# Turning float64 weights into fp32 on VectorE and ScalarE instead of GpSimd, and computing a branch's flag beside the last block

## The chip, the core and the metric

The kernel runs on one core of a Trainium2 chip. The metric is the device time of one execution in microseconds (us). The engines are named as in the profile: PE (TensorE, the matmuls), PEld (its weight loads), DVE (VectorE), ACT (ScalarE), POOL (GpSimd) and SP (SyncE, which here issues the input DMAs). Each engine works through its own list of instructions in order, and waits at an instruction until the semaphores that it names have been raised.

## The reference

A gated linear recurrence over the sequence, followed by a feed-forward block on its output. Cut to what is computed:

```
q, k, v, f_logit: (4, 8, 768, 48) float32      # batch, heads, sequence, head width
f = sigmoid(f_logit)
for t in range(768):
    state = f[t][:, None] * state + outer(k[t], v[t])   # per batch and head, 48 x 48
    y[t] = q[t] @ state
x = y as (3072, 384)                            # tokens x (heads * width)
g = x @ w_gate;  out = (g * sigmoid(g) * (x @ w_val)) @ w_out
w_gate, w_val: (384, 1536), w_out: (1536, 384), all three float64
```

The weights come as float64 (two 32-bit words each), and the kernel makes fp32 of them on the chip.

## The kernel before

The sequence is cut into `NCH` = 6 chunks of 128 tokens. A unit is one chunk of one batch element, so a chunk has 4 units. For each unit `attention` has five steps: transposes of f, k and q on PE (L442), sigmoid on ACT (L447), two scans on DVE over the chunk (L452 "tails" and L462 "head", which turn the recurrence into one masked product), scores `sc` on PE (L478), their mask `A` on DVE (L480), the output `y` and the new state `dS` on PE (L495, L498, L505), a copy of the state on DVE (L511, L513), and the transposed output `xT` (L521, L522). POOL multiplies the old state by the chunk's decay (L470, "decayed").

`mlp(c)` then works on the 512 tokens of chunk c. For each of the 12 column blocks j it has a gate product and a value product (L539), Silu on ACT (L546) and a multiplication on DVE (L550); afterwards 4 `down` products (L555), a copy on ACT (L558) and the output DMA (L560). The code interleaves `mlp(c)` with `attention(c + 1)`. A list scheduler then sets the order on each engine; the order that it gives is fixed when the kernel is built.

The weights are cut into 18 pieces of 128 x 768 numbers. `fetch` loads a piece's float64 words into one of three buffers `w64` (tile `w`, issued by SP at L387); `convert` makes fp32 of it. Four pieces are converted during `attention(0)` by the order of the code, and one after each of the column blocks of `mlp(0)`. So all conversion lies in the first fifth of the execution, and from chunk 1 on the weights lie in SBUF as fp32. A conversion takes the high words `hi` and the low words `lo` and has, in its form before, nine instructions: five on DVE (L393, L399, L400, L401, L403), two on ACT (L395, L397) and two on POOL (L402, L404). The tile `sign` between ACT and POOL has one buffer (`bufs=1`).

Whether the short form of the recurrence is accurate enough is known only from the data: `least` collects the smallest decay. After `short_path`, the kernel reduces it to one flag (a reduction on DVE, a transpose on PE, two small DVE instructions), every engine loads the flag into a register (TENSOR_LOAD, L635) and branches (L636): if the flag is set, `general_path` does all again in a longer way. With these inputs it isn't set.

Of the kernel before, what the change touches and what calls it, by code (L numbers as in the profile page):

```python
# [1 line left out]

# [283 lines left out]


@with_exitstack
def short_path(ctx, tc, least, q, k, v, f_logit, moe_w_gate, moe_w_val, moe_w_out, out):

# [8 lines left out]
    nc = tc.nc  # L299
    B, H, S, D = q.shape  # L300
    C = 128
    NCH = S // C
# [8 lines left out]
    NRAW = 3  # L311
# [6 lines left out]
    wst = ctx.enter_context(tc.tile_pool(name="wst", bufs=2))  # L318
# [4 lines left out]
    ident = const.tile([128, 128], FP32, tag="ident", name="ident")  # L323
# [43 lines left out]
    def load(u):  # L367
        b, c = units[u]
        rows = slice(c * C, (c + 1) * C)
        for nm, src in (("f", f_logit), ("k", k), ("q", q)):  # L370
            nc.sync.dma_start(out=raw[nm][u % NRAW][:, :, 0:D], in_=src[b, :, rows, :].rearrange("h t d -> t h d"))
        vt[u] = att.tile([128, H, D], FP32, tag="v", name="v", bufs=6)
        nc.sync.dma_start(out=vt[u], in_=v[b, :, rows, :].rearrange("h t d -> t h d"))

    def weight_piece(dst, src):

        if src.dtype == FP32:  # L380
            return (lambda: nc.sync.dma_start(out=dst, in_=src)), (lambda: None)
        shape = list(dst.shape)
        kept = {}

        def fetch():
            kept["w"] = wst.tile(shape[:2] + [2 * shape[2]], I32, tag="w64", name="w64", bufs=3)
            nc.sync.dma_start(out=kept["w"], in_=src)  # L387

        def convert():
            words = kept["w"].rearrange("p a (n two) -> p a n two", two=2)  # L390
            lo, hi = words[:, :, :, 0], words[:, :, :, 1]
            top = wst.tile(shape, I32, tag="top", name="top")
            nc.vector.tensor_single_scalar(top, hi, (1 << 20) - 1, op=ALU.bitwise_and)  # L393
# [3 lines left out]
            nc.scalar.activation(sign, hi, AF.Sign)  # L397
            p2 = wst.tile(shape, I32, tag="p2", name="p2")
            nc.vector.tensor_scalar(p2, hi, 20, 0x7FF, op0=ALU.logical_shift_right, op1=ALU.bitwise_and)  # L399
            nc.vector.tensor_scalar(p2, p2, 1023 - 127, 1023 + 128, op0=ALU.max, op1=ALU.min)  # L400
            nc.vector.tensor_scalar(p2, p2, 1023 - 127, 1 << 23, op0=ALU.subtract, op1=ALU.mult)  # L401
            nc.gpsimd.tensor_tensor(sign, sign, p2.bitcast(FP32), ALU.mult)  # L402
            nc.vector.scalar_tensor_tensor(man, lo.bitcast(U32), 2.0 ** -52, man, op0=ALU.mult, op1=ALU.add)  # L403
            nc.gpsimd.tensor_tensor(dst, man, sign, ALU.mult)  # L404

        return fetch, convert

    per = 2 if moe_w_gate.dtype != FP32 else 1

    def in_rows(w):  # L410
        return w.rearrange("(a p) n -> p a n", p=128)
# [165 lines left out]

    for u in range(NRAW):
        load(u)

    def weights():
        if fetches:
            fetches.pop(0)()
        if converts:
            converts.pop(0)()

    for i, f in enumerate(attention_steps(0)):
# [12 lines left out]
    assert not fetches and not converts  # L600


@with_exitstack
def kernel(
    ctx: ExitStack,
    tc: tile.TileContext,
    q: bass.AP,
    k: bass.AP,
    v: bass.AP,
    f_logit: bass.AP,  # L610
    moe_w_gate: bass.AP,
    moe_w_val: bass.AP,
    moe_w_out: bass.AP,
    out: bass.AP,
):
# [7 lines left out]
    short_path(tc, least, *args)  # L623
    low = flags.tile([128, 1], FP32, tag="low", name="low")
    nc.vector.tensor_reduce(low, least, axis=mybir.AxisListType.X, op=ALU.min)
    with tc.tile_pool(name="flagp", bufs=1, space=bass.MemoryType.PSUM) as pool:
        ident = flags.tile([128, 128], FP32, tag="idf", name="idf")
        make_identity(nc, ident)
        row = pool.tile([1, 128], FP32, tag="row", name="row")
# [3 lines left out]
    flag = flags.tile([1, 1], I32, tag="flag", name="flag")  # L633
    nc.vector.tensor_single_scalar(flag, one, LEAST, op=ALU.is_lt)
    redo = nc.values_load(flag[0:1, 0:1], min_val=0, max_val=1, skip_runtime_bounds_check_because="a comparison")  # L635
    with tc.If(redo > 0):  # L636
        general_path(tc, *args)


# [30 lines left out]
```

## Time and profile before

| what | value |
|---|---|
| median of 3 runs | 803.4 us (800.85 to 803.81) |
| the profiled execution | 797.71 us |
| its span, first to last instruction | 796.0 us |
| PE busy | 739.0 us (93%) |
| DVE busy | 296.8 us (37%) |
| ACT busy | 183.0 us (23%) |
| POOL busy | 96.6 us (12%) |
| mean granted TensorE clock | 0.952 |

The span lies 1.7 us under the profiled execution's own time. A busy share is an average over the whole span; the first fifth, in which weights are converted, looks quite different from the rest, so stages are read apart in what follows. The stages are marked by PE's first gate product of each chunk: 69.48 us for chunk 0, 220.77 us for chunk 1, and then 340.81, 460.85, 580.89 and 696.45 us.

### The profile page before, as it was taken

How to read it: one execution, taken by the hardware profiler on the slowest of the kernel's cores; microseconds unless marked ns; L12 is line 12 of the kernel's file. 1: busy time of each engine (PE TensorE's matmuls, PEld its weight loads, DVE VectorE, ACT ScalarE, POOL GpSimd, SP SyncE). 2: the span in 40 equal slices, each digit the busy share in tenths (PEclk: the TensorE clock that was granted, in tenths of full speed). 3: DMA queues.
4: the chain of work that ended last, by engine and by line, in shares of the span. 5: the costliest groups of instructions: out<-in, count | busy, mean ns of one | idle time of the engine just before them, and what ended most of it. 6: DMA issues, size and time to landing. Idle time of an engine off the chain costs nothing.

```text
span 796.0 us, 7687 instructions
## 1 busy us (share of the span) xinstructions
PE 739.0 (93%) x3129; PEld 433.5 (54%) x3129; DVE 296.8 (37%) x430; ACT 183.0 (23%) x264; POOL 96.6 (12%) x79
## 2 busy tenths in 40 slices
PE   5558694899999999999999999999999999999996
PEld 4545352556655555655555655555655555644453
DVE  6887999951033430133431133431133330011100
ACT  2323343441032230132230132230132221011100
POOL 2245566520000000000000000000000000000000
PEclk9656898799999999999999999999999999999999
DMA  9744534301112111112111112111010000000000
GB/s 218 192 128 112 157 107 138 80 19 33 30 40 40 38 22 30 31 40 40 32 28 30 30 40 40 24 27 30 21 41 0 1 1 10 21 10 1 0 20 26
DMA packets 109772, 38.34 MB, mean 48 GB/s; under 512 B 100512, under 2 KB 103584, under 8 KB 109728
## 3 DMA queue, kind: packets, MB, share of 16 engines
q1 hardware_dynamic: 106272, 33.04, 17.7%
q10 hardware_dynamic: 3456, 4.72, 1.7%
q8 instruction: 27, 0.44, 0.2%
q14 instruction: 17, 0.14, 0.1%
HBM read 33.03 MB, written 4.72 MB: 47 GB/s over the span
## 4 chain that ended last, share of the span: by engine, by line
PE 82%; DVE 12%; issue 2%; ACT 2%; POOL 2%; DMA 0%; DVEq 0%; POOLq 0%
PE o L555 23%; PE gate L539 21%; PE val L539 21%; PE y L498 5%; PE sc L478 3%; DVE p L399 3%; PE y L495 2%; PE dS L505 2%; DVE top L393 2%; DVE head L462 1%; DVE p L400 1%; DVE top L403 1%; PE kt L485 1%; PE fTp L442 1%; PE kTp L442 1%
## 5 line engine op out<-in xcount | busy, mean ns | idle before, releaser
L539 PE MATMUL gate<-xT,w_gate 128*128 128x512 f32 x432 | 201.9, 604 | 1.4 <-ACT xT L522 0.6
L539 PE MATMUL val<-xT,w_val 128*128 128x512 f32 x432 | 199.3, 597 | 0.0
L555 PE MATMUL o<-w_out,h 128*128 128x384 f32 x576 | 188.8, 487 | 0.0
L555 PEld LDWEIGHTS o<-w_out,h 128*128 128x128 f32 x576 | 108.3, 190 | 73.2 <-issue 0.5
L539 PEld LDWEIGHTS gate<-xT,w_gate 128*128 128x128 f32 x432 | 80.4, 194 | 89.5 <-issue 86.2
L539 PEld LDWEIGHTS val<-xT,w_val 128*128 128x128 f32 x432 | 79.3, 191 | 85.1 <-issue 83.6
L550 DVE TENSOR_TENSOR h<-h,val 128x512 f32<-128x512 f32 x72 | 49.3, 684 | 189.0 <-PE val L539 188.0
L546 ACT ACTIVATE h<-gate 128x512 f32<-128x512 f32 x72 | 42.8, 596 | 206.7 <-PE gate L539 206.5
L470 POOL TENSOR_TENSOR decayed<-state,tails 128x384 f32<-128x384 f32 x20 | 17.1, 856 | 479.8 <-DVE tails L452 479.8
L498 PE MATMUL y<-v,A 128*128 128x48 f32 x384 | 59.5, 285 | 9.5 <-DVE A L480 9.5
L480 DVE TENSOR_TENSOR A<-sc,causal 128x512 f32<-128x512 f32 x48 | 30.9, 685 | 94.9 <-PE sc L478 94.9
L498 PEld LDWEIGHTS y<-v,A 128*128 128x128 f32 x384 | 55.4, 211 | 10.6 <-DVE A L480 10.3
L478 PE MATMUL sc<-qT,kT 48*128 48x128 f32 x384 | 32.6, 318 | 29.3 <-DVE qT L465 29.3
L452 DVE TENSOR_TENSOR_SCAN tails<-gates,ones 128x516 f32<-128x516 f32 x24 | 29.6, 1231 | 78.2 <-ACT gates L447 78.2
L558 ACT COPY ob<-o 128x384 f32<-128x384 f32 x24 | 11.5, 478 | 180.8 <-PE o L555 180.8
L478 PEld LDWEIGHTS sc<-qT,kT 48*128 48x128 f32 x384 | 27.4, 216 | 44.4 <-DVE qT L465 32.2
L402 POOL TENSOR_TENSOR sign<-sign,p 128x768 f32<-128x768 f32 x18 | 38.1, 2115 | 71.3 <-DVE p L401 62.0
L495 PE MATMUL y<-decayed,qT 128*128 128x96 f32 x160 | 33.9, 295 | 6.9 <-DVE A L480 6.9
L462 DVE TENSOR_TENSOR_SCAN head<-gates,starts 128x516 f32<-128x516 f32 x24 | 38.0, 1584 | 0.7
L495 PEld LDWEIGHTS y<-decayed,qT 128*128 128x128 f32 x160 | 26.7, 198 | 15.7 <-issue 14.4
L511 DVE TENSOR_TENSOR state<-decayed,dS 64x192 f32<-64x192 f32 x32 | 11.2, 351 | 59.4 <-PE dS L505 59.1
L447 ACT ACT_TABLE_LOAD x20 | 25.7, 1283 | 15.3 <-PE fTp L442 13.4
(58 smaller groups left out, 464.9 us busy)
## 6 DMA issues: line engine op xcount, KB each, us to landing
fraw<-in_f_logit_dram SPq DMA_DIRECT2D x24, 192.0 KB, 2.7
kraw<-in_k_dram SPq DMA_DIRECT2D x24, 192.0 KB, 2.6
qraw<-in_q_dram SPq DMA_DIRECT2D x24, 192.0 KB, 3.2
v<-in_v_dram SPq DMA_DIRECT2D x24, 192.0 KB, 3.2
w<-in_moe_w_gate_dram SPq DMA_DIRECT2D x6, 768.0 KB, 4.4
w<-in_moe_w_val_dram SPq DMA_DIRECT2D x6, 768.0 KB, 4.9
w<-in_moe_w_out_dram SPq DMA_DIRECT2D x6, 768.0 KB, 4.2
out_dram<-ob ACTq DMA_DIRECT2D x24, 192.0 KB, 1.8
```

Source lines behind the costliest of these rows:

```text
L402: nc.gpsimd.tensor_tensor(sign, sign, p2.bitcast(FP32), ALU.mult)
L447: nc.scalar.activation(pairs(gate)[:, :, 1:N1], p, AF.Sigmoid)
L452: nc.vector.tensor_tensor_scan(tail[:, 0:n][:, ::-1], gate[:, 0:n][:, ::-1], ones[:, ::-1], 1.0, op0=ALU.mult, op1=ALU.add)
L462: nc.vector.tensor_tensor_scan(head, gate[:, 0:n], start, 1.0, op0=ALU.mult, op1=ALU.add)
L478: nc.tensor.matmul(sc[par][:, a * C:(a + 1) * C], lhsT=kT[r, a, :], rhs=qT[r, a, :], start=True, stop=True)
L480: nc.vector.tensor_tensor(A[:, par], sc[par].rearrange("p (a t) -> p a t", t=C), causal.unsqueeze(1).broadcast_to((128, HP, C)), ALU.mult)
L495: nc.tensor.matmul(both, lhsT=qT[:, a, :], rhs=decayed[:, a, :, :].rearrange("p r d -> p (r d)"), start=True, stop=False, skip_group_check ...
L498: nc.tensor.matmul(both[:, par * D:(par + 1) * D], lhsT=A[:, par, a, :], rhs=vt[u][:, 2 * a + par, :], start=(c == 0), stop=True, skip_gro ...
L539: nc.tensor.matmul(p, lhsT=w[:, i, j * 128:(j + 1) * 128], rhs=xT[c][:, i, :], start=(i == 0), stop=(i == KT - 1))
L546: nc.scalar.activation(h[j], p, AF.Silu)
L550: nc.vector.tensor_tensor(h[j], h[j], p, ALU.mult)
L555: nc.tensor.matmul(p, lhsT=h[j][:, b * C:(b + 1) * C], rhs=w_out[:, j, :], start=(j == 0), stop=(j == NF - 1))
```

## The change

`convert` is written anew. ACT now does its two instructions first, straight from the loaded words: `up` is the low word scaled by 2^-29 and rounded to an integer (L395), `top` is the absolute value of the high word (L397). DVE then clamps `top` (as a float, L398), shifts it into the place of an fp32 number (L400), puts the sign and the top bit of the exponent on it (L401), and adds `up` as a 32-bit integer, so that the sum's bits are the fp32 number (L402). POOL has no part in it, and the tiles `sign`, `p2` and `man` are gone. The fetches and conversions during `attention(0)` are set at slightly different steps. The second part: the reductions that give the flag stand in a function `judge`, which is called after `mlp(4)` with `attention(5)`, before `mlp(5)`; the load of the flag and the branch stand where they stood. The identity matrix that `judge` needs is now made ahead of `short_path`.

Line numbers rise by one in the code behind the new import, and by up to six at the end (L480 becomes L481, L635 becomes L638).

```diff
         def convert():
             words = kept["w"].rearrange("p a (n two) -> p a n two", two=2)
             lo, hi = words[:, :, :, 0], words[:, :, :, 1]
+            up = wst.tile(shape, I32, tag="up", name="up")
+            nc.scalar.activation(up, lo.bitcast(U32), AF.Copy, scale=2.0 ** -29)
             top = wst.tile(shape, I32, tag="top", name="top")
-            nc.vector.tensor_single_scalar(top, hi, (1 << 20) - 1, op=ALU.bitwise_and)
-            man = top.bitcast(FP32)
-            nc.scalar.activation(man, top, AF.Identity, bias=1.0, scale=2.0 ** -20)
-            sign = wst.tile(shape, FP32, tag="sign", name="sign", bufs=1)
-            nc.scalar.activation(sign, hi, AF.Sign)
-            p2 = wst.tile(shape, I32, tag="p2", name="p2")
-            nc.vector.tensor_scalar(p2, hi, 20, 0x7FF, op0=ALU.logical_shift_right, op1=ALU.bitwise_and)
-            nc.vector.tensor_scalar(p2, p2, 1023 - 127, 1023 + 128, op0=ALU.max, op1=ALU.min)
-            nc.vector.tensor_scalar(p2, p2, 1023 - 127, 1 << 23, op0=ALU.subtract, op1=ALU.mult)
-            nc.gpsimd.tensor_tensor(sign, sign, p2.bitcast(FP32), ALU.mult)
-            nc.vector.scalar_tensor_tensor(man, lo.bitcast(U32), 2.0 ** -52, man, op0=ALU.mult, op1=ALU.add)
-            nc.gpsimd.tensor_tensor(dst, man, sign, ALU.mult)
+            nc.scalar.activation(top.bitcast(FP32), hi.bitcast(FP32), AF.Abs)
+            nc.vector.tensor_scalar(top.bitcast(FP32), top.bitcast(FP32), as_float(0x38000000), as_float(0x47F00000),
+                                    op0=ALU.max, op1=ALU.min)
+            nc.vector.tensor_scalar(top, top, 3, 0x3FFFFFFF, op0=ALU.logical_shift_left, op1=ALU.bitwise_and)
+            nc.vector.scalar_tensor_tensor(top, hi, -(1 << 30), top, op0=ALU.bitwise_and, op1=ALU.bitwise_or)
+            nc.vector.tensor_tensor(dst.bitcast(I32), top, up, ALU.add)
...
     for i, f in enumerate(attention_steps(0)):
         f()
-        if i in (2, 4, 6):
+        if i in (2, 3, 5):
             fetches.pop(0)()
-        if i in (10, 13, 16, 19):
+        if i in (11, 14, 16, 18):
             weights()
...
         take_turns(pieces, attention_steps(c + 1) if c + 1 < NCH else [])
+        if c == NCH - 2:
+            judge(bank)
...
+    def judge(bank):
+        low = flags.tile([128, 1], FP32, tag="low", name="low")
+        nc.vector.tensor_reduce(low, least, axis=mybir.AxisListType.X, op=ALU.min)
+        row = bank("row")[0:1, 0:128]
         nc.tensor.transpose(row, low, ident)
         one = flags.tile([1, 1], FP32, tag="one", name="one")
         nc.vector.tensor_reduce(one, row, axis=mybir.AxisListType.X, op=ALU.min)
...
+    short_path(tc, least, judge, *args)
+    with tc.If(redo[0] > 0):
         general_path(tc, *args)
```

What the scheduler makes of it shows in three places. The first is DVE between the product `qT` and the mask `A` of unit 2, the third unit of chunk 0 (`w_226` and `w_259` are loaded pieces of float64 words, `p_386` and `p_452` the tile `p2`). Before:

```order
L465 TENSOR_TENSOR qT<-qTp,head 128x512
L393 TENSOR_SCALAR top<-w_226 128x768
L399 TENSOR_SCALAR p_386<-w_226 128x768
L400 TENSOR_SCALAR p_386<-p_386 128x768
L403 SCALAR_TENSOR_TENSOR top<-w_226,top 128x768
L401 TENSOR_SCALAR p_386<-p_386 128x768
L393 TENSOR_SCALAR top<-w_259 128x768
L399 TENSOR_SCALAR p_452<-w_259 128x768
L480 TENSOR_TENSOR A<-sc,causal 128x512 x2
```

The same stretch of DVE after:

```order
L466 TENSOR_TENSOR qT<-qTp,head 128x512
L400 TENSOR_SCALAR top<-top 128x768
L401 SCALAR_TENSOR_TENSOR top<-w_209,top 128x768
L402 ISA w_val<-top,up 128x3x512
L398 TENSOR_SCALAR top<-top 128x768
L481 TENSOR_TENSOR A<-sc,causal 128x512 x2
```

Seven instructions of conversion stood between the two, now four. The integer add is listed as ISA, over 3 x 512 elements per partition for 3 x 256 numbers: it goes over halves of 16 bits.

The second place is DVE in the next unit, unit 3, from the scan `head` to the mask `A` (`w_334`, `w_379` are pieces, `p_513`, `p_538` the tile `p2`). Before:

```order
L462 SCALAR_TENSOR_TENSOR head<-gates_104,starts_108 128x516
L393 TENSOR_SCALAR top<-w_334 128x768
L465 TENSOR_TENSOR qT<-qTp,head 128x512
L399 TENSOR_SCALAR p_513<-w_334 128x768
L400 TENSOR_SCALAR p_513<-p_513 128x768
L403 SCALAR_TENSOR_TENSOR top<-w_334,top 128x768
L401 TENSOR_SCALAR p_513<-p_513 128x768
L393 TENSOR_SCALAR top<-w_379 128x768
L399 TENSOR_SCALAR p_538<-w_379 128x768
L400 TENSOR_SCALAR p_538<-p_538 128x768
L480 TENSOR_TENSOR A<-sc,causal 128x512 x2
```

The same stretch of DVE after:

```order
L463 SCALAR_TENSOR_TENSOR head<-gates_109,starts_113 128x516
L466 TENSOR_TENSOR qT<-qTp,head 128x512
L398 TENSOR_SCALAR top<-top 128x768
L400 TENSOR_SCALAR top<-top 128x768
L401 SCALAR_TENSOR_TENSOR top<-w_344,top 128x768
L481 TENSOR_TENSOR A<-sc,causal 128x512 x2
```

Eight instructions of conversion stood in that stretch, now three. Ahead of `head`, between this unit's `kT` and `head`, stood L401 and L403 of a piece; now one L402 stands there.

The third place is PE at the end of the program, where `o` are the last down products and `row` is the transpose for the flag. Before:

```order
L539 MATMUL gate<-xT,w_gate 128x512 x3
L539 MATMUL val<-xT,w_val 128x512 x3
L555 MATMUL o<-w_out,h 128x384 x48
L630 MATMUL row<-idf,low 1x128
L635 TENSOR_LOAD flag
L636 COMPARE_AND_BRANCH
```

After, the transpose stands at the start of `mlp(5)`, between the last `xT` and the first gate product:

```order
L556 MATMUL o<-w_out,h 128x384 x12
L522 MATMUL xTp<-ident,x 128x128 x3
L633 MATMUL row<-idf,low 1x128
L540 MATMUL gate<-xT,w_gate 128x512 x3
L540 MATMUL val<-xT,w_val 128x512 x3
```

PE's list now ends with the 48 down products, the load of the flag and the branch. On DVE the reduction to `one` and the comparison moved ahead of the last 12 multiplications `h`; on every engine the load of the flag and the branch are still last. On POOL the 36 instructions of the conversion are gone, and the making of the identity `idf` stands ahead of that of `ident`. On SP the order of the loads around the first seven pieces is the same.

More of the change, by code (lines that the diff above doesn't have):

```diff
@@ L1 @@
+import struct
 from contextlib import ExitStack
@@ L288, in short_path @@
 @with_exitstack
-def short_path(ctx, tc, least, q, k, v, f_logit, moe_w_gate, moe_w_val, moe_w_out, out):
+def short_path(ctx, tc, least, judge, q, k, v, f_logit, moe_w_gate, moe_w_val, moe_w_out, out):
     nc = tc.nc
@@ L391, in convert, with as_float @@
             lo, hi = words[:, :, :, 0], words[:, :, :, 1]
+            up = wst.tile(shape, I32, tag="up", name="up")
+            nc.scalar.activation(up, lo.bitcast(U32), AF.Copy, scale=2.0 ** -29)
             top = wst.tile(shape, I32, tag="top", name="top")
[L393 to L404 removed]
+            nc.scalar.activation(top.bitcast(FP32), hi.bitcast(FP32), AF.Abs)
[4 more added lines that the diff above has]
+            nc.vector.tensor_tensor(dst.bitcast(I32), top, up, ALU.add)
         return fetch, convert
+    def as_float(bits):
+        return struct.unpack("<f", struct.pack("<I", bits))[0]
     per = 2 if moe_w_gate.dtype != FP32 else 1
@@ L575, in take_turns @@
             g()
-    for u in range(NRAW):
-        load(u)
     def weights():
@@ L585, in weights @@
             converts.pop(0)()
+    for u in range(NRAW):
+        load(u)
     for i, f in enumerate(attention_steps(0)):
         f()
-        if i in (2, 4, 6):
+        if i in (2, 3, 5):
             fetches.pop(0)()
-        if i in (10, 13, 16, 19):
+        if i in (11, 14, 16, 18):
             weights()
@@ L622 @@
     least = flags.tile([128, HP], FP32, tag="least", name="least")
[L623 to L629, printed above, removed]
+    ident = flags.tile([128, 128], FP32, tag="idf", name="idf")
+    make_identity(nc, ident)
+    redo = []
+    def judge(bank):
+        low = flags.tile([128, 1], FP32, tag="low", name="low")
+        nc.vector.tensor_reduce(low, least, axis=mybir.AxisListType.X, op=ALU.min)
+        row = bank("row")[0:1, 0:128]
         nc.tensor.transpose(row, low, ident)
@@ L632 @@
         nc.vector.tensor_reduce(one, row, axis=mybir.AxisListType.X, op=ALU.min)
[L633 to L636, printed above, removed]
+        flag = flags.tile([1, 1], I32, tag="flag", name="flag")
+        nc.vector.tensor_single_scalar(flag, one, LEAST, op=ALU.is_lt)
+        redo.append(nc.values_load(flag[0:1, 0:1], min_val=0, max_val=1,
+                                   skip_runtime_bounds_check_because="a comparison"))
+    short_path(tc, least, judge, *args)
+    with tc.If(redo[0] > 0):
         general_path(tc, *args)
```

## The prediction

> **What bounds the kernel now.** First the page's 40 slices (each 19.9 us), for the stages:
>
> ```profile
> PE   5558694899999999999999999999999999999996
> DVE  6887999951033430133431133431133330011100
> POOL 2245566520000000000000000000000000000000
> PEclk9656898799999999999999999999999999999999
> ```
>
> From the ninth slice on PE is full at full clock. Before that PE has gaps, DVE stands at nine tenths in four slices, POOL works there and nowhere else, and the granted clock dips. So I cut the span at PE's marks (columns: length, busy time and instructions of PE, PEld, DVE, ACT, POOL, granted clock, DMA share, GB/s):
>
> ```profile
> 20.00:69.50 49.50, 29.61 (x195) 26.53 (x196) 38.84 (x52) 13.94 (x21) 21.07 (x10) 0.58 0.57 151
> 69.50:160.34 90.84, 70.64 (x264) 39.90 (x264) 89.51 (x99) 35.80 (x46) 53.50 (x28) 0.86 0.43 118
> 160.34:220.77 60.43, 59.86 (x279) 36.95 (x278) 13.04 (x23) 11.66 (x21) 4.39 (x3) 1.00 0.11 27
> 220.77:340.81 120.04, 119.96 (x540) 69.98 (x541) 33.94 (x56) 27.66 (x40) 3.33 (x4) 1.00 0.16 34
> ```
>
> The last row is a chunk without conversion: 120.04 us, PE never idle. The chunk with conversion, rows two and three, has the same PE work and takes 151.27 us; for its first 90.84 us DVE is 98.5% busy and PE idles 20.2 us. DVE bounds it, and what makes DVE so busy shows instruction by instruction (shortest, median, longest in ns):
>
> ```profile
> L393 DVE TENSOR_SCALAR top<-w x18: 528/602/2170, 23.2 to 158.0; 128x768 int32<-128x768 int32 x18
> L399 DVE TENSOR_SCALAR p<-w x18: 545/2156/2174, 23.7 to 147.7; 128x768 int32<-128x768 int32 x18
> L400 DVE TENSOR_SCALAR p<-p x18: 528/560/2165, 28.3 to 158.4; 128x768 int32<-128x768 int32 x18
> L401 DVE TENSOR_SCALAR p<-p x18: 529/549/562, 30.8 to 159.0; 128x768 int32<-128x768 int32 x18
> L403 DVE SCALAR_TENSOR_TENSOR top<-w,top x18: 920/950/2565, 28.9 to 159.5; 128x768 f32<-128x768 uint32 x18
> L402 POOL TENSOR_TENSOR sign<-sign,p x18: 1804/1998/2447, 31.5 to 159.7; 128x768 f32<-128x768 f32 x18
> L397 ACT ACTIVATE sign<-w x18: 889/912/961, 19.9 to 157.0; 128x768 f32<-128x768 int32 x18
> ```
>
> The same instruction takes 0.55 or 2.17 us. The timeline (start, duration) says when:
>
> ```profile
> 39.99 2.02 POOL L404 TENSOR_TENSOR w_val<-top,sign 128x768 f32<-128x768 f32 x1
> 40.26 1.27 DVE L480 TENSOR_TENSOR A<-sc,causal 128x512 f32<-128x512 f32 x2
> 54.81 0.55 DVE L399 TENSOR_SCALAR p<-w 128x768 int32<-128x768 int32 x1
> 57.43 1.99 POOL L402 TENSOR_TENSOR sign<-sign,p 128x768 f32<-128x768 f32 x1 [3.56 <-DVE p L401]
> 57.67 2.17 DVE L399 TENSOR_SCALAR p<-w 128x768 int32<-128x768 int32 x1
> 59.50 2.00 POOL L404 TENSOR_TENSOR w_val<-top,sign 128x768 f32<-128x768 f32 x1
> ```
>
> At 54.81 POOL is idle and L399 takes 0.55 us. At 57.67 POOL has just begun; L399 ends at 59.84, 0.42 us after POOL's 59.42. DVE's work between SBUF tiles stands still until POOL's instruction is over. The mask A, which reads PSUM, runs beside POOL unhindered.
>
> **The change, part by part.** The marks on the path of chunk 0, and PE's first gate products:
>
> ```profile
> 22.01 1.29 DVE L480 TENSOR_TENSOR A<-sc,causal 128x512 f32<-128x512 f32 x2 [1.84 <-PE sc L478]
> 27.55 0.69 DVE L457 TENSOR_TENSOR kT<-kTp,tails 128x512 f32<-128x512 f32 x1
> 31.29 0.68 DVE L465 TENSOR_TENSOR qT<-qTp,head 128x512 f32<-128x512 f32 x1
> 47.29 0.69 DVE L457 TENSOR_TENSOR kT<-kTp,tails 128x512 f32<-128x512 f32 x1 [0.32 <-PE kTp L442]
> 49.45 2.83 DVE L462 TENSOR_TENSOR_SCAN head<-gates,starts 128x516 f32<-128x516 f32 x1
> 54.94 2.08 PE L478 MATMUL sc<-qT,kT 48*128 48x128 f32 x16 [6.20 <-DVE qT L465]
> 61.84 1.27 DVE L480 TENSOR_TENSOR A<-sc,causal 128x512 f32<-128x512 f32 x2
> 69.48 3.90 PE L539 MATMUL gate<-xT,w_gate 128*128 128x512 f32 x6
> 220.77 2.84 PE L539 MATMUL gate<-xT,w_gate 128*128 128x512 f32 x6
> ```
>
> Prices of the new DVE instructions. L398 and L400 have one tensor input, like L393 to L401: 0.55 us. L401 has two, like L403: 0.95 us. The add L402 has no row. It goes over 1536 halves of 16 bits; if two go through per step it costs what L403 costs, 0.95; if one, 768 more steps of 1.04 ns (0.95 less the 0.68 of 512 elements in the row of qT, over 256), so 1.75. I take 0.95, since its bytes are those of L403, and keep 0.95 to 1.75. Four instructions make 3.0 us, less some 0.08 of overlap each: 2.7 a piece. The five before sum to 3.05 by their shortest and to 4.8 by their medians in the rows above. So it isn't the instruction saved that counts but the standing still.
>
> [...] No instruction of this trace has 16-bit operands.
>
> *Term A, up to the first gate product at 69.48.* Unit 2, from the end of qT (31.97) to A (40.26): 8.3 us, seven conversion instructions in the way. Now L400, L401, L402 and L398, 2.7 us, somewhat over the 2.08 that PE needs for the scores. Gain 5.5. Unit 3, from kT (47.29) to A (61.84): 14.55 us. Now kT 0.69, three short ones 0.4, L402 0.95, head 1.23 (its shortest; it waits 1.6 for POOL here), qT 0.68, then L398, L400, L401 2.05: 6.0 less overlaps 0.6, 5.4. Gain 9.1. The time between, A at 40.26 to kT at 47.29, is PE's y and dS at half clock (7.03 us); unit 1 needed 5.54 at a better clock (22.01 to 27.55), and the stretch from A to the end of xT shortens likewise. With less idling the clock may recover: 0 to 4 us, I take 1.5. The fetches hide: a piece lands 4.1 to 6.7 us after its issue and is asked for three pieces ahead. Sum 16.1 (13 to 18.6); first gate product at 53.4.
>
> [...]
>
> *Term B, chunk 0's products beside chunk 1's attention, 151.29 us.* Five pieces are done by then; 13 remain. DVE needs 13 times 2.7 to 3.0 beside the 33.94 of a chunk: 73 of 120 us. ACT has two instructions a piece as before, each near the 0.91 of L397, 13 times 1.8 beside 27.66: 51. Both fall below PE, which sets 120.04. I add 1.5 for the cold start (3.90 against 2.84) and small waits: 121.5, gain 29.8. Unknown is what the order on DVE costs, where h waits behind conversions; if each of the 13 pieces shows PE its longest instruction, it is 130. Gain 21.3 to 31.25. POOL's removed 36 instructions save nothing of their own, and L470 stays.
>
> What the conversion's first instruction on ACT waited for, what SP's fetches waited for, and the landing of pieces:
>
> ```profile
> ACT sign L397 <- POOL w_gate L404: 14.0, 4, 5.6
> SPq L387 <- DVE top L403: 75.0, 15, 8.6
> DMA to landing us min/median/max: 4.1/4.4/6.7
> ```
>
> Before, L397 waited for POOL to give `sign` back (w_val and w_out likewise). Now L395 waits for the landing and for DVE to give `up` back, two pieces earlier; behind it on ACT stand the copies of kt and xT and Silu, for which PE waits. DVE's 2.7 us a piece against PE's 120 us for 13 pieces makes that wait the shorter one. Fetches wait for DVE, not for memory; 13 pieces of 768 KB and four units of as much in 121 us ask some 110 GB/s, under the 151 of the earlier stage.
>
> *Term C, the flag.* The tail:
>
> ```profile
> L635 PEldq TENSOR_LOAD <-flag x1: 485/485/485, 790.1 to 790.1; - x1
> L635 ACTq TENSOR_LOAD <-flag x1: 482/482/482, 790.4 to 790.4; - x1
> L636 PEldq COMPARE_BRANCH  x1: 4226/4226/4226, 790.7 to 790.7; - x1
> L636 ACTq EVENT_SEMAPHORE  x1: 17/17/17, 794.4 to 794.4; - x1
> L636 PEldq EVENT_SEMAPHORE  x1: 51/51/51, 795.0 to 795.0; - x1
> ```
>
> The long part, the branch of 4.23 us on PE, stays. PE can load the flag 0.6 us sooner, but ACT, which loads it after its last output DMA, ends at 794.4 as before. Gain 0.6 (0 to 1). The moved transpose lies where PE waits for the copy of xT anyway; DVE's two small steps and the flag's place there cost nothing, as DVE has 86 us to spare per chunk.
>
> Sum: 16.1 + 29.8 + 0.6 = 46.5. The profiled execution, 797.7, becomes 751.2, its span 749.5. The runs' median is 803.4, 5.7 above that execution; the same gain puts it at 756.9.
>
> **The rivals.**
> *One half per step.* The add costs 1.75. In term A two adds lie on the path, 1.6; in term B up to 13 times 0.8. Between 758 and 769, middle 763. Nothing in this profile speaks against it.
> *DVE still sets the pace in term B*, by its order, not its load: half of the 31.25 stays. 803.4 - 16.1 - 15.6 - 0.6 = 771. Against it: DVE has 40% to spare.
> *The add is slow: slower than before.* Decided by its price. If none of it is hidden, the gain is gone when 18 adds cost 46.5 more, at 3.5 us each; if the 47 us that DVE has free in term B hide their part, at 6.1. At 8 us, 757 + 18 x 7.05 - 47 = 837. For it only that no row shows this instruction; POOL, slower at two inputs, needs 2.0 (L402).
> *POOL was not the cause.* The long instances stay, and with four instructions for five the time stays about 802. Against it stand the rows at 54.81 and 57.67.
>
> **How the numbers follow.** The forecast 0.76; one half per step 0.10; DVE's order 0.08; slow add 0.03; POOL not the cause 0.03. The forecast's bounds, gains of 34.3 to 50.8, give 752.6 to 769.1; the second rival adds 771 above, and below I allow the 2.5 us by which the runs' lowest lies under their median: 750 to 771. 0.5% is 4 us, about what a measurement of this kernel can tell. Faster holds the first three cases, 0.94; same 0.03; slower 0.03.
>
> **What would show it.** L398 and L400 near 0.55 us with hardly a long instance, L401 near 0.95, L402 near 0.95 (or 1.75). POOL busy some 21 us. The first gate product at 50 to 56, chunk 1's at 172 to 183, 120.04 us a chunk after that. The tail 0.6 shorter. Wrong it would be if L402 took over 2 us, if PE waited in term B for h or for weights, or if the long instances stayed without POOL.

## The result and the profile after

The changed kernel takes 754.65 us (median of 4 runs, 753.33 to 757.35) against 803.05 us before: a ratio of 0.9406, 95% interval 0.9373 to 0.9439. Run again beside the later experiments it took 755.58 us against 798.43 for the kernel before, 0.9459 (0.9429 to 0.9489). The prediction was 756.9, 0.942 of the median that it started from. The profiled execution went from 797.71 to 754.08 us, its span from 796.0 to 752.3.

The 40 slices of the page after (now 18.8 us each), and the shares of the chain that ended last:

```profile
PE   6689999999999999999999999999999999999997
POOL 2000000000000000000000000000000000000000
PEclk9859999999999999999999999999999999999999
PE 96%; DVE 2%; ACT 1%; DMA 0%; issue 0%; DVEq 0%
```

PE is full from the fourth slice on, not from the ninth, and POOL stays under a tenth after the first. The new instructions on DVE (shortest, median, longest in ns):

```profile
L398 DVE TENSOR_SCALAR top<-top x18: 530/552/561, 25.4 to 131.6; 128x768 f32<-128x768 f32 x18
L400 DVE TENSOR_SCALAR top<-top x18: 547/557/561, 26.0 to 132.9; 128x768 int32<-128x768 int32 x18
L401 DVE SCALAR_TENSOR_TENSOR top<-w,top x18: 931/957/960, 29.5 to 133.5; 128x768 int32<-128x768 int32 x18
L402 DVE CUSTOM_DVE_ANT_0 w_gate<-top,up x6: 926/950/959, 32.0 to 103.2; 128x1536 uint16<-128x1536 uint16 x6
```

Not one of them has a long instance: where L399 had a median of 2156 ns and a shortest of 545, the longest is now within 6% of the shortest. The integer add goes over 1536 halves of 16 bits and takes 0.95 us, as long as L401 takes for 768 numbers (0.96): twice as many elements in the same time.

Chunk 0's products beside chunk 1's attention, and the chunk after it, cut at PE's first gate products (columns as in the table of before: length, then busy time of PE, PEld, DVE, ACT, POOL, then granted clock, DMA share, GB/s):

```profile
57.81:178.53 120.72, 120.64 (x542) 70.30 (x541) 70.50 (x110) 47.91 (x66) 3.48 (x4) 0.99 0.39 108
178.53:298.60 120.07, 119.99 (x541) 70.02 (x541) 33.95 (x56) 27.67 (x41) 3.33 (x4) 1.00 0.15 33
```

A chunk with conversion now costs 0.65 us more than one without; before it cost 31.2 more. DVE's 102.55 us beside these products became 70.50.

The marks in chunk 0:

```profile
32.88 0.68 DVE L466 TENSOR_TENSOR qT<-qTp,head 128x512 f32<-128x512 f32 x1
36.40 1.28 DVE L481 TENSOR_TENSOR A<-sc,causal 128x512 f32<-128x512 f32 x2
43.53 0.69 DVE L458 TENSOR_TENSOR kT<-kTp,tails 128x512 f32<-128x512 f32 x1 [0.26 <-PE kTp L443]
49.55 1.29 DVE L481 TENSOR_TENSOR A<-sc,causal 128x512 f32<-128x512 f32 x2
57.81 3.51 PE L540 MATMUL gate<-xT,w_gate 128*128 128x512 f32 x6
```

Three stages make up the 43.6 us between the two spans: 11.7 up to the first gate product (69.48 to 57.81), 30.6 from there to chunk 1's (151.29 to 120.72), and 1.4 behind it, nearly all of it in the tail. The tail after:

```profile
L638 PEldq TENSOR_LOAD <-flag x1: 487/487/487, 741.3 to 741.3; - x1
L638 ACTq TENSOR_LOAD <-flag x1: 483/483/483, 748.2 to 748.2; - x1
L642 PEldq COMPARE_BRANCH  x1: 3647/3647/3647, 741.9 to 741.9; - x1
L642 ACTq EVENT_SEMAPHORE  x1: 17/17/17, 751.5 to 751.5; - x1
L642 PEldq EVENT_SEMAPHORE  x1: 51/51/51, 747.3 to 747.3; - x1
```

PE's sequencer loads the flag at 741.3 and branches at 741.9, while down products that it has already queued run on until 747.2. PE's branch, which was the last long thing of the kernel before, lies wholly beside matmuls; ACT's path sets the end now.

### The profile page after: what moved, and what is told of

It is laid out like the page before. It is cut to its first block, busy times and chain, and to the rows that moved or that the text cites. A ratio compares the mean times of both kernels' runs of the same rounds, so it can differ in the third digit from the quotient of the medians.

```text
span 752.3 us, 7603 instructions
## 1 busy us (share of the span) xinstructions
PE 730.3 (97%) x3129; PEld 428.7 (57%) x3129; DVE 252.5 (34%) x412; ACT 183.1 (24%) x264; POOL 21.0 (3%) x43
## 4 chain that ended last, share of the span: by engine, by line
PE 96%; DVE 2%; ACT 1%; DMA 0%; issue 0%; DVEq 0%
PE gate L540 25%; PE val L540 25%; PE o L556 25%; PE y L499 6%; PE sc L479 4%; PE y L496 3%; PE dS L506 2%; PE kt L486 2%; PE kTp L443 2%; PE fTp L443 1%; PE qTp L443 1%; PE xTp L522 1%; DVE head L463 1%; DVE qT L466 0%; DMA fraw<-in_f_logit_dram 0%; DVE kT L458 0%
## 5 line engine op out<-in xcount | busy, mean ns | idle before, releaser
L540 PE MATMUL gate<-xT,w_gate 128*128 128x512 f32 x432 | 199.3, 597 | 0.8 <-ACT xT L523 0.5
L481 DVE TENSOR_TENSOR A<-sc,causal 128x512 f32<-128x512 f32 x48 | 30.9, 685 | 93.3 <-PE sc L479 93.2
L479 PE MATMUL sc<-qT,kT 48*128 48x128 f32 x384 | 30.6, 304 | 11.7 <-DVE qT L466 11.7
L479 PEld LDWEIGHTS sc<-qT,kT 48*128 48x128 f32 x384 | 25.7, 204 | 26.8 <-DVE qT L466 13.1
L463 DVE TENSOR_TENSOR_SCAN head<-gates,starts 128x516 f32<-128x516 f32 x24 | 34.1, 1420 | 0.7
L458 DVE TENSOR_TENSOR kT<-kTp,tails 128x512 f32<-128x512 f32 x24 | 16.5, 689 | 27.9 <-PE kTp L443 27.7
```

The source lines that it names most:

```text
L463: nc.vector.tensor_tensor_scan(head, gate[:, 0:n], start, 1.0, op0=ALU.mult, op1=ALU.add)
L479: nc.tensor.matmul(sc[par][:, a * C:(a + 1) * C], lhsT=kT[r, a, :], rhs=qT[r, a, :], start=True, stop=True)
L481: nc.vector.tensor_tensor(A[:, par], sc[par].rearrange("p (a t) -> p a t", t=C), causal.unsqueeze(1).broadcast_to((128, HP, C)), ALU.mult)
L540: nc.tensor.matmul(p, lhsT=w[:, i, j * 128:(j + 1) * 128], rhs=xT[c][:, i, :], start=(i == 0), stop=(i == KT - 1))
```

## The experiments

Each group of runs has its own runs of the kernel before beside it, and a ratio is against those. Where times of one group are compared, that is said.

Theory: DVE's SBUF instructions stood still during POOL's two multiplies a piece; without POOL, DVE's work fits beside PE's. Rivals: it was the number of DVE's instructions; DVE's order or a slow add still holds PE; and part of the gain is the flag's.

**The two parts by themselves.** The new `convert` and its steps in the kernel before, the flag at the end:

```diff
+            up = wst.tile(shape, I32, tag="up", name="up")
+            nc.scalar.activation(up, lo.bitcast(U32), AF.Copy, scale=2.0 ** -29)
...
+            nc.vector.tensor_tensor(dst.bitcast(I32), top, up, ALU.add)
...
-        if i in (10, 13, 16, 19):
+        if i in (11, 14, 16, 18):
```

> The new conversion and its steps, with the flag's reductions at the end as before. Theory: the conversion gave everything but the tail. From the last down product to the span's end the changed kernel took 5.0 us and the kernel before 6.5, so this one should lie 1.5 us above the changed kernel's 754.7, at 756.2, with 6.5 us of tail, a first gate product near 58 and chunk 1's near 178. Rival: the flag's place is worth nothing, and the 1.5 us came from elsewhere in the chunks: 754.7.

Measured: 759.78 us (757.61 to 760.07), 0.9475 (0.9435 to 0.9515). In its profile the first gate product is at 61.93, chunk 1's 120.40 later, and the tail 6.7 us. The other way round, the flag as after with the old conversion:

```diff
-    short_path(tc, least, *args)
-    low = flags.tile([128, 1], FP32, tag="low", name="low")
...
+        if c == NCH - 2:
+            judge(bank)
...
+    short_path(tc, least, judge, *args)
```

> The old conversion and its steps, with the flag's reductions ahead of the last block. Theory: only the tail shortens, by 1.5 us: 803.1 becomes 801.6, with the first gate product near 69 and chunk 1's near 221, and 5.0 us from the last down product to the end. Rival: 0.6 us at most, as predicted, since ACT's load of the flag and its branch still follow the last output copy: 802.5.

Measured: 795.5 us (794.2 to 799.31), 0.9942 (0.9918 to 0.9967), with a tail of 5.0 us. The conversion carries 42 us of the gain (0.0525 of 800.87), the flag alone 4.6 (2.6 to 6.6). The tails are those expected, but the flag alone gains 3 us more than its tail, past the expectation of the theory, and the conversion alone lies 0.0016 to 0.0069 over the changed kernel's two ratios, 1.3 to 5.5 us: with its first gate product 4 us later, it speaks for neither. Both kernels also differ from their neighbours in the order of chunk 0, which the scheduler sets anew after such an edit. The cleaner test of the flag is further down.

**The old conversion without POOL.**

```diff
-            nc.gpsimd.tensor_tensor(sign, sign, p2.bitcast(FP32), ALU.mult)
+            nc.vector.tensor_tensor(sign, sign, p2.bitcast(FP32), ALU.mult)
...
-            nc.gpsimd.tensor_tensor(dst, man, sign, ALU.mult)
+            nc.vector.tensor_tensor(dst, man, sign, ALU.mult)
```

> The kernel before with its nine instructions, only that the two multiplies of POOL (L402, L404) are issued on DVE. Theory (DVE stood still for POOL): no instruction of the conversion takes 2.17 us any more. DVE's seven cost 3.05 + 2 x 0.95 = 4.95 us a piece; in the 120 us of PE work of chunk 0's products that is 13 x 4.95 + 34 = 98 us, so PE sets the pace: chunk 1's first gate product comes about 121 us after chunk 0's. Chunk 0 itself has two more instructions a piece on DVE than the kernel before has and ends between 60 and 66 us. Total 763 to 770. Rival (it was the number of DVE's instructions, five against four): seven are worse than five, 18 x 1.9 = 34 us more of DVE work, 803 to 837.

Measured: 762.05 us (761.72 to 766.62), 0.9527 (0.9478 to 0.9575). L399, whose median was 2156 ns before, L403, whose longest was 2565, one of the moved multiplies, and the stage of chunk 0's products:

```profile
L399 DVE TENSOR_SCALAR p<-w x18: 522/552/583, 25.9 to 149.9; 128x768 int32<-128x768 int32 x18
L403 DVE SCALAR_TENSOR_TENSOR top<-w,top x18: 925/952/977, 30.2 to 153.1; 128x768 f32<-128x768 uint32 x18
L402 DVE TENSOR_TENSOR sign<-sign,p x18: 941/952/996, 33.3 to 153.9; 128x768 f32<-128x768 f32 x18
60.84:185.57 124.73, 121.40 (x541) 70.22 (x540) 95.94 (x157) 49.13 (x68) 4.64 (x4) 0.99 0.37 102
```

DVE issues seven instructions a piece instead of five and is busy for 95.94 us in this stage, less than the 102.55 it needed with five and POOL beside it. The run also takes POOL out of the chain of a piece, so that nothing waits for POOL's results any more; but a wait is not busy time, and it is DVE's busy time that fell. That is what the theory expected, 1 us under its range in all, with the stage at 124.7 rather than 121: two edited words bring 38 us (0.0473 of 800.87), the larger part of the gain. Four instructions instead of these seven and the flag are worth the rest, 5 to 10 us by the changed kernel's two ratios.

**POOL put back beside the new conversion.**

```diff
             nc.vector.scalar_tensor_tensor(top, hi, -(1 << 30), top, op0=ALU.bitwise_and, op1=ALU.bitwise_or)
+            idle = wst.tile(shape, FP32, tag="idle", name="idle", bufs=1)
+            for _ in range(2):
+                nc.gpsimd.tensor_tensor(idle, up.bitcast(FP32), up.bitcast(FP32), ALU.mult)
             nc.vector.tensor_tensor(dst.bitcast(I32), top, up, ALU.add)
```

> The changed kernel, with two POOL multiplies of 128 x 768 a piece put beside DVE's four instructions; they read up, write a tile that nobody reads, and nothing waits for them except for the buffer of up. Theory (DVE stands still for POOL): L398, L400, L401 and the add show instances of 2 us and more again. POOL has 13 x 2 x 2.0 = 52 us of such work beside chunk 0's products; if all of it stops DVE, DVE has 13 x 2.7 + 34 + 52 = 121 us there, just PE's 120, so the time rises by what the order costs, 5 to 25 us, to between 760 and 780. Rival (POOL was not the cause, the shorter chain was): nothing on the chain has changed, 754.7, and the durations stay at 0.55 and 0.95.

Measured: 778.77 us (778.62 to 779.46), 0.9722 (0.9683 to 0.976): half of the gain is gone. DVE's clamp, POOL's multiplies, and the stage:

```profile
L398 DVE TENSOR_SCALAR top<-top x18: 529/1147/1826, 26.2 to 156.4; 128x768 f32<-128x768 f32 x18
L404 POOL TENSOR_TENSOR idle<-up x36: 1465/1661/2283, 22.6 to 153.4; 128x768 f32<-128x768 f32 x36
66.15:203.13 136.98, 128.06 (x541) 73.87 (x541) 93.86 (x110) 47.06 (x66) 48.53 (x30) 0.94 0.35 95
```

And one stretch of the timeline, POOL's four multiplies in a row with DVE beside them:

```profile
83.99 6.68 POOL L404 TENSOR_TENSOR idle<-up 128x768 f32<-128x768 f32 x4 [5.32 <-ACT up L395]
85.79 1.28 DVE L484 TENSOR_TENSOR A<-sc,causal 128x512 f32<-128x512 f32 x2
87.53 1.82 DVE L398 TENSOR_SCALAR top<-top 128x768 f32<-128x768 f32 x1
89.27 2.22 DVE L401 SCALAR_TENSOR_TENSOR top<-w,top 128x768 int32<-128x768 int32 x1
91.41 0.68 DVE L554 TENSOR_TENSOR h<-h,val 128x512 f32<-128x512 f32 x1
92.01 0.55 DVE L400 TENSOR_SCALAR top<-top 128x768 int32<-128x768 int32 x1
```

POOL works from 83.99 to 90.67. Inside that, L398 and L401 take 1.82 and 2.22 us; once it is over, L400 takes 0.55. The mask A, which reads PSUM, is at its usual 1.28 in the middle of it. With the same 110 instructions as after, DVE's busy time in the stage rises by 23.4 us for POOL's 45 more: about half of POOL's time falls on an instruction of DVE that it stops. The stage is 16.3 us longer (136.98 against 120.72), and chunk 0's gate product comes 8.3 us later, at 66.15. Nothing waits for what POOL computes; only the buffer of `up` is held until POOL has read it. By the profile that cost nothing in this stage: ACT waited nine times, 42.1 us in all, to write `up` again, and each of these waits ended with DVE's add, none with POOL. So the longer stage comes by way of DVE's longer instructions.

**What a slower add would have cost.** The add issued twice, then four times a piece (n is 1 and 3):

```diff
+            more = wst.tile(shape, I32, tag="more", name="more", bufs=1)
+            for _ in range(n):
+                nc.vector.tensor_tensor(more, top, up, ALU.add)
             nc.vector.tensor_tensor(dst.bitcast(I32), top, up, ALU.add)
```

> The changed kernel with its integer add of 0.95 us issued twice a piece, the first into a tile that nobody reads. Theory (DVE has room beside PE): in the 120 us of chunk 0's products DVE then has 13 x (2.7 + 0.9) + 34 = 81 us, all hidden; in chunk 0 two adds lie on the path, 1.8 us. Ratio to the kernel before 0.942 to 0.945 against the changed kernel's 0.941, that is 756 to 759. Rival (DVE's order lets PE wait for each piece): 13 x 0.9 = 11.7 more beside the 1.8, a ratio of 0.957, 768.

> The same with three more adds, so that a piece's adds cost 3.8 us. Theory: DVE has 13 x (2.7 + 2.7) + 34 = 104 us beside PE's 120, still hidden but for waits; in chunk 0 two pieces lie on the path, 5.5 us, and a third in part. 760 to 770, with the first gate product at 63 to 68 and chunk 1's 120 to 126 us after it. Rival (nothing is hidden, the break-even of 3.5 us an add that was reckoned with 18 adds on the path): 18 x 2.7 = 49 more, 800 and over.

Measured: 758.61 us (756.15 to 759.37), 0.9474 (0.9434 to 0.9513), and 763.45 (761.59 to 766.38), 0.9555 (0.9515 to 0.9595). The stage of chunk 0's products with two adds:

```profile
60.62:183.51 122.89, 121.94 (x541) 70.73 (x540) 82.69 (x124) 47.72 (x66) 4.63 (x4) 0.98 0.40 107
```

and with four:

```profile
61.40:186.05 124.65, 121.54 (x542) 69.77 (x541) 106.37 (x157) 48.10 (x66) 6.87 (x4) 1.00 0.38 102
```

With 106.37 us of DVE work beside PE's 121.5 the stage is only 3.9 us longer than after: 13 pieces with 2.85 us more each are 37 us, and nine tenths of them are hidden. An add of 3.8 us, past the break-even of 3.5 predicted for the case that nothing is hidden, still gives a ratio of 0.956.

**PE kept busy in chunk 0.** The first stage of the changed kernel ended 4.4 us later than predicted, and from 32 to 59 us PE worked at half clock. Products of 128 x 512 that nobody reads were set into the gaps, `n` of them per unit (3, 7 and 4, set in units 0, 1, 2 ahead of the scores of the next):

```diff
+        if u in n:
+            warm = fps.tile([128, 512], FP32, tag="m", name="warm")
+            for _ in range(n[u]):
+                nc.tensor.matmul(warm, lhsT=x[:, 0:128], rhs=ones[:, 0:512], start=True, stop=True)
         p = bank("xTp")
```

> The changed kernel with 14 matmuls of 128 x 512 that nobody reads, where PE waits for DVE in chunk 0: 3 ahead of unit 1's scores, 7 ahead of unit 2's, 4 ahead of unit 3's. In the changed kernel the granted clock was half from 32.1 to 59.4 us; of these 27 us PE worked about 20. Theory (PE's gaps bring the half clock, and it is what the first stage came out short by): the half clock is shorter or gone, the work of those 20 us takes 10 to 15, and some 5 to 8 us of it lies on the path. First gate product at 50 to 53, 747 to 750 in all. Rival (the half clock has nothing to do with the gaps): the stretch of half clock stays as it is, the 14 products take 0.9 us each in it, 6.4 + 3.7 us against the two larger gaps of 4.4 and 2.5, and the time rises by 2 to 4 us, to 757 to 759.

From the start:

```diff
+    first = fps.tile([128, 512], FP32, tag="m", name="warm")
+    for _ in range(8):
+        nc.tensor.matmul(first[:, 0:128], lhsT=ident, rhs=ident, start=True, stop=True)
     for u in range(NRAW):
         load(u)
...
+        if u == 0:
+            warm = fps.tile([128, 512], FP32, tag="m", name="warm")
+            for _ in range(3):
+                nc.tensor.matmul(warm, lhsT=kT[:, 0, :], rhs=ones[:, 0:512], start=True, stop=True)
         A = att.tile([128, 2, HP, C], FP32, tag="A", name="A")
```

> The one before, and also 8 small products (128 x 128) ahead of the first transposes and 3 of 128 x 512 ahead of unit 0's scores. In the changed kernel's profiled execution the first granted full clock is recorded at 21.8 us, in that of the kernel before at 10.4, and unit 1's scores ended 2 us later for it. Theory (the program begins at half clock, and the clock rises only once PE has been busy for some time, at a point that differs between executions): full clock by 10 to 14 us in each, 1 to 3 us less than with PE kept busy in the later gaps alone, 745 to 749, and the runs lie closer together. Rival (where the clock first rises does not hang on PE's work): the same as with the later gaps alone, or 1 to 3 us longer, as the 3 products ahead of unit 0's scores cost 0.9 us each at half clock.

Measured: 752.29 us (749.27 to 756.33), 0.9413 (0.9376 to 0.945), and 753.9 (752.81 to 755.34), 0.942 (0.9391 to 0.9449). The rows that show the clock are PE's 14 products of y, which take 1.76 us at full clock and 3.22 at half. In the changed kernel, for units 0 to 3, with the wait ahead of unit 2's scores:

```profile
14.77 3.22 PE L499 MATMUL y<-v,A 128*128 128x48 f32 x14
25.52 1.76 PE L499 MATMUL y<-v,A 128*128 128x48 f32 x14 [0.17 <-DVE A L481]
33.62 2.08 PE L479 MATMUL sc<-qT,kT 48*128 48x128 f32 x16 [4.39 <-DVE qT L466]
38.41 3.22 PE L499 MATMUL y<-v,A 128*128 128x48 f32 x14
52.26 3.22 PE L499 MATMUL y<-v,A 128*128 128x48 f32 x14
```

With the 14 products in the gaps:

```profile
30.57 6.17 PE L523 MATMUL warm<-ones,x 128*128 128x512 f32 x14
37.01 1.16 PE L479 MATMUL sc<-qT,kT 48*128 48x128 f32 x16
41.69 2.04 PE L499 MATMUL y<-v,A 128*128 128x48 f32 x14
53.31 1.76 PE L499 MATMUL y<-v,A 128*128 128x48 f32 x14
56.76 2.84 PE L544 MATMUL gate<-xT,w_gate 128*128 128x512 f32 x6
```

So the gaps did bring the half clock: filled, the scores take 1.16 us instead of 2.08 and y 1.76 to 2.04 instead of 3.22. The rows also show why so little came of it: one such product is two passes and takes 0.9 us (14 passes in 6.17 us for the 7 of the first row), twice what I had reckoned, and 7 of them put unit 2's scores off by 3.4 us. With 11 more products from the very start, unit 0's y takes 1.76 us at 14.71 where it took 3.22 at 14.77. That the program begins at half clock shows in the trace of the kernel before, of the changed kernel in both its profiles, and of the conversion alone, the flag last and three forms with added products (the first four transposes take 1.06 to 1.09 us, four at full clock 0.60 to 0.66). That PE's work raises it is not shown: the first full clock is recorded at 7.0 us here, but at 7.0 in the execution of the kernel before too, without such products (the 10.4 of the expectation is where it first fell back there). Those products put unit 0's scores off from 9.97 to 11.93 as well.

Half as many (1, 4 and 2 in the gaps; 4 and 1 for 8 and 3 at the start), with the changed kernel beside them in one group:

> The changed kernel itself once more, as the measure for the three others of this group. 753 to 757, a ratio of 0.941 to 0.946; the theory of the clock says that its executions differ by when PE's first full clock comes, so that they spread over 3 to 4 us.

> PE kept busy in chunk 0 with half as many products: 1, 4 and 2 ahead of the scores of units 1, 2 and 3. The 14 of the fuller form took 0.9 us each at full clock, twice what I had reckoned, and put unit 2's scores off from 33.6 to 37.0 us. Theory: 4 x 0.9 = 3.6 and 2 x 0.9 = 1.8 us fit the gaps of 4.4 and 2.5, the clock stays full for most of units 2 and 3, and nothing is put off: first gate product at 53 to 55, 3 to 4 us under the changed kernel of this group. Rival (less than full cover doesn't hold the clock): half clock from about 32 to 59 as in the changed kernel, and the same time or 1 us more.

> The one before, with 4 small products ahead of the first transposes and 1 of 128 x 512 ahead of unit 0's scores. With 8 and 3 of them the first full clock came at 6.8 us instead of 22, but they put the first transposes off by 1.7 us and unit 0's scores by 2. Theory: half of them raise the clock before 14 us and put nothing off: 1 to 3 us under the one with the later gaps alone. Rival: too little to raise the clock sooner, the same time.

Measured in one group: the changed kernel 755.58 us (753.24, 753.36, 757.8, 757.89), 0.9459 (0.9429 to 0.9489); PE kept busy less 751.74 (749.49 to 751.94), 0.9405 (0.9387 to 0.9423); the same from the start 753.1 (752.75 to 753.66), 0.9429 (0.9415 to 0.9443). The second is the best kernel of this study, 3.8 us under the changed one of its group, and its interval lies clear of that one's. The changed kernel's first ratio, 0.9406, is no larger, because the kernel before was slower in that group; in microseconds the four runs lie under all eight of the changed kernel (753.24 to 757.89). Its rows:

```profile
14.51 1.76 PE L499 MATMUL y<-v,A 128*128 128x48 f32 x14
35.48 1.76 PE L499 MATMUL y<-v,A 128*128 128x48 f32 x14
47.98 3.22 PE L499 MATMUL y<-v,A 128*128 128x48 f32 x14
53.53 3.49 PE L544 MATMUL gate<-xT,w_gate 128*128 128x512 f32 x6
```

The first gate product is at 53.53. In this execution the clock rose by 14.5 us, ahead of the first added product, so part of its 749.49 us is that execution's own; the three others lie near 751.8. The additions at the start again brought no gain: 1.4 us more here and 1.6 in the fuller form, with intervals that overlap.

**The flag by itself.** The changed kernel's program with the reductions behind the last product; PE's and DVE's orders are the same up to chunk 5:

```diff
-    short_path(tc, least, judge, *args)
+    short_path(tc, least, lambda bank: None, *args)
+    with tc.tile_pool(name="flagp", bufs=1, space=bass.MemoryType.PSUM) as pool:
+        judge(lambda name: pool.tile([128, 512], FP32, tag=name, name=name))
```

> The changed kernel with the flag's transpose and its two small DVE instructions behind the last down product again, in a PSUM pool of their own; the identity stays ahead of the program, so that every engine's order up to the last chunk's products is the changed kernel's. Theory: the flag is worth its tail alone, 1.5 us over the changed kernel of this group, with the two first gate products at the same times. Rival (the 4 to 5 us between the changed kernel and the conversion alone, and between the flag alone and the kernel before, are the flag's): 4 to 5 us over.

Measured: 758.49 us (756.87 to 759.76), 0.9495 (0.9474 to 0.9516), 2.9 over the changed kernel of this group. The tail of its profile, in which every engine waits for the flag:

```profile
L638 ACTq TENSOR_LOAD <-flag x1: 481/481/481, 749.5 to 749.5; - x1
L644 PEldq COMPARE_BRANCH  x1: 4327/4327/4327, 749.8 to 749.8; - x1
L644 ACTq EVENT_SEMAPHORE  x1: 17/17/17, 753.6 to 753.6; - x1
```

From the last down product, which ends at 748.5, to the span's end at 755.1 it is 6.6 us, against 5.1 after (747.2 to 752.3): 1.5, the theory's figure. Chunk 0's stage of products is 120.73 long against 120.72. What the times show beyond 1.5 sits ahead of the first gate product, where the two kernels have the same order on PE: there the executions differ by the clock (first recorded full at 26.5 us against 21.8). Whether the flag is worth more than its tail, up to the 4.6 us of the flag alone, the times leave open; no row shows a second effect of it.

## Why the prediction came out right, and where it was off

**Term B**, predicted 121.5 us for the stage and a gain of 29.8: measured 120.72 and 30.6. Its steps held one by one: L398 and L400 at 0.55, L401 at 0.96, the add at 0.95, DVE 70.50 us (predicted 73), ACT 47.91 (51), POOL 21.0 over the whole span (21). The 1.5 us for a cold start and small waits was 0.65. One figure of the range was added wrongly: 13 longest instructions of 0.95 on 120.04 give 132.4, not 130, and a least gain of 18.9; the measured 30.6 is far from either.

**The add.** Of the prices 0.95 and 1.75 the first is the measured one: L402 takes 926 to 959 ns. The rival of one half per step is out by that row. Had it come true, the kernel with two adds shows about what it would have cost: 758.6 us, the lower end of the 758 to 769 given for it, since the stage of the products hides most of it. The rival of DVE's order fails by the same stage, and more so with four adds, where 106 us of DVE work made it 3.9 us longer. "POOL was not the cause" fails twice, by the old conversion without POOL and by the new one with POOL beside it.

**Term A** was mis-sized: gain 11.7 instead of 16.1, with the first gate product at 57.81, outside the 50 to 56 named as its sign. The DVE stretches were right. From qT's end to A, unit 2: 33.56 to 36.40, 2.84 us after 8.29, gain 5.45 (predicted 5.5). From kT to A, unit 3: 6.02 after 14.55, gain 8.5 (9.1). The step that failed is the clock's recovery, put at +1.5 in a range from 0 to 4: both were an estimate that no run shows, and what the runs show in its place is a granted clock of 0.50 from 32.0 to 59.4 us. Without the 1.5, 14.0 would have remained, and the stage gained 2.3 less than even that. In the rows: unit 2's qT ends 1.6 us later than before (33.56 against 31.97), since unit 0's y ran at half clock in this execution, 3.22 us where it took 1.76 in that of the kernel before; from A to the next kT it is 7.13 against 7.03, where I had expected less; and from A of unit 3 to the gate product 8.26 against 7.64. With 14 us of DVE's stretches gone, PE still idled 4.39 and 2.46 us ahead of two units' scores, and the clock was half from 32 to 59 us. By what the fuller and the lesser filling of these gaps did, that was the gaps' doing. The lower end of the range, 0, was no bound: it left out that the clock's first rise differs between executions (at 21.8 and at 32.9 us in the two profiles of the changed kernel). The trace's clock records have it full from 21.8 to 32.1 us and half to 59.4, for 10.24 and 27.31 us; the shortest of the records in the trace of the kernel before is 3.41 us long (7.0 to 10.4), and these two lengths are 3 and 8 times that. Windows of the changed kernel, cut close to steps of this length:

```profile
28.70:32.10 3.40, 0.54 (x5) 0.29 (x3) 3.39 (x9) 1.08 (x2) 0.00 (x0) 0.99 0.94 187
35.50:38.90 3.40, 3.40 (x21) 3.09 (x19) 3.29 (x6) 1.18 (x2) 0.00 (x0) 0.50 0.76 245
38.90:42.30 3.40, 3.40 (x23) 3.29 (x23) 1.45 (x2) 0.48 (x1) 0.00 (x0) 0.50 0.28 55
56.00:59.40 3.40, 3.35 (x10) 2.44 (x11) 3.12 (x5) 2.03 (x4) 0.00 (x0) 0.51 0.03 2
59.40:62.80 3.40, 3.40 (x9) 1.52 (x8) 3.30 (x7) 2.58 (x4) 0.83 (x1) 1.00 0.94 276
```

PE is busy for 0.54 of 3.40 us in the first, and the clock halves at its end. In the next two rows PE is busy throughout, with small products, and the clock stays half; only after the fourth, with the 512 columns of the gate product in it, is it full again, as the last row shows. What in the fourth window brought the clock back, the runs leave open: PE is as busy in the two before it (3.40 of 3.40 us) as in the fourth (3.35).

**Term C** was predicted at 0.6 and measured 1.4 us (6.5 to 5.1), past its bound of 1. That PE's branch leaves the path and ACT's own load and branch set the end came out as said. The step that failed is that ACT would end as it did before: from its load of the flag to its last row above it took 4.0 us (790.4 to 794.4) and now takes 3.3 (748.2 to 751.5). In the three traces whose flag rows are shown it goes with when the engines branch: 3.3 us in the changed kernel, where they load the flag at different times (SP and POOL at 654.2 us, DVE at 716.4, PE at 741.3, ACT at 748.2); 4.0 in the kernel before and 4.1 with the flag last (749.5 to 753.6), where all five engines load it within 0.3 us. Why, no run shows.

**The base.** The profiled execution should have become 751.2 and was 754.08; the terms were 2.9 too large in sum (4.4 too much in A, 0.8 too little in each of B and C). The forecast of 756.9 came out 2.3 over the median all the same, since it added the gain to a median of three runs, 5.7 above the profiled execution. That closeness is luck: a gain reckoned too large from a base that was too high for it. The mechanism, and the sizes of B and of the DVE stretches in A, are not. The kernel before lies anywhere from 797.7 to 803.8 from one execution to the next.

## What to carry to other kernels

When one instruction has a shortest time and a median four times as long, look for what another engine was doing at that moment before counting instructions: here moving two multiplies from POOL onto the busier engine gained 38 us. Work on POOL beside DVE's SBUF work cost DVE about half of POOL's time here (23.4 of 45 us), even where nothing waited for POOL's results. When waits are removed ahead of PE, look at what gaps stay: with two of 2.5 and 4.4 us the clock stayed at half, and seven products that nobody reads, cut to fit the gaps, gained 3.8.

## What the runs showed of the hardware

PE begins this program at half clock (its first four transposes take 1.09 us in both profiles of the changed kernel, against 0.60 at full clock), and where it first rises differs. With the same order on PE, unit 1's scores were done at full clock in one execution (1.16 us, at 22.98) and at half in another; in the profile of the changed kernel run again:

```profile
22.86 2.08 PE L479 MATMUL sc<-qT,kT 48*128 48x128 f32 x16 [1.65 <-DVE qT L466]
61.30 1.06 PE L540 MATMUL gate<-xT,w_gate 128*128 128x512 f32 x1
```

Here the first full clock is recorded at 32.9 us and the first gate product comes at 61.30; in the profile shown above it was 21.8 and 57.81, and in that of the flag set last 26.5 and 59.09. Of the 3.8 us between the two executions of the changed kernel, 3.5 lie ahead of that product. These three first records, with one order on PE up to there, spread over 11 us; with other orders the first lies at 7.0 us in the kernel before and at 42.4 in the conversion alone. The page of the profile doesn't show it: its row of the clock counts the time ahead of the first record as full, and so has a 9 for the first 18.8 us of the changed kernel, in which unit 0's y took the 3.22 us of half clock.

In the changed kernel PE's sequencer loaded the flag and branched while products that it had queued still ran, 5.9 us ahead of the end of the last of them (741.3 to 747.2). PE's branch took 4.23 us before, 4.33 with the flag last and 3.65 after the change, where it lies beside matmuls (741.9 to 745.5) and off the path, since the flag is there early.
